# Attention followed by a two-layer product on one core: both transpositions of a unit ahead of both copies, the score stream carried into the next batch, fewer dummy products

## The chip, the cores and the metric

The kernel runs on one core of a Trainium2 chip. Times are device microseconds. A time is the median of several executions. A profile is one further execution, recorded by the hardware profiler; its own time and its span (first to last instruction) are given beside the median. The engines are named PE (TensorE: matrix products), PEld (its weight loads), DVE (VectorE), ACT (ScalarE), POOL (GpSimd) and SP (SyncE); the last two mainly issue transfers here.

## What is computed

Attention with a squared ReLU in place of the softmax, over 8 batches, 12 heads, 448 positions and 64 values a head, and then two matrix products with a squared ReLU between them, on 3,584 rows.

```python
def _attn_ref(q, k, v):                      # (8, 12, 448, 64) each
    S = q.shape[2]
    scale = 1.0 / np.sqrt(q.shape[-1])
    scores = scale * np.matmul(q, k.transpose(0, 1, 3, 2))
    attn = np.maximum(scores, 0.0) ** 2 / S
    return np.matmul(attn, v).astype(np.float32)

def _moe_ref(x, w_in, w_out):                # (3584, 768), (768, 2048), (2048, 768)
    h = x @ w_in
    r = np.maximum(h, 0.0)
    g = r * r
    return (g @ w_out).astype(np.float32)
```

The output of the attention, with heads side by side, is the `x` of the second function.

## The kernel before

**Units and tiles.** A batch is three units of four heads. A unit's keys are cut into seven pieces, so a unit has seven tiles and a batch 21: batch 0 is tiles 0 to 20, batch 1 tiles 21 to 41, and so on. One tile is, for four heads, 64 keys against 448 queries: four score products on PE (line 203, `score`), a ReLU out of PSUM on ACT (line 220 for one tile while the first PSUM layout stands, line 214 for a pair of tiles in the second), a square on DVE (line 230), and four products with v (line 244, `av_round`) which add up over the unit's seven tiles in one PSUM tile `avt`, of which there is a single buffer. At the unit's last tile `avt` is copied to `xt` (line 258 on DVE; for unit 2 line 252 on ACT and line 254 on DVE, a half each). These products with v are called average rounds below.

**Transposing q and k.** Scores need q and k with the head's values on the partitions. For units 0 to 5 PE does it, in `pe_transpose`: 14 transpositions of q into PSUM (line 179), a copy out on DVE (line 186, tile `qT`), then 14 of k and a copy out (tile `kT`). Both halves lie in one PSUM tile, a `slot`. For unit 0 the copy of k is ACT's (line 183). From unit 6 on, q and k are loaded in float32, cast on POOL (line 109) and transposed by a transfer issued from SP (line 121).

**The PSUM layouts.** While batch 0's attention runs, PSUM holds `avt` and three slots of two banks. Then the slots are closed, and two banks `mm` for the products and one score tile `s` of four banks take their place. The later `pe_transpose` calls use that one score tile as their slot.

**Order.** The order is written out by hand. The dummy products (`warm`, line 169: zeros times zeros, 448 columns) come first, with unit 0's transpositions among them. Then batch 0's tiles are run in pairs by `visit`: scores of the pair with their ReLU, then up to three average rounds of earlier tiles, then the squares of the pair. Units 1, 2 and 3 are transposed ahead of pairs 2 and 5 and behind the last. Then come the steps: for each pair of batches, 96 products of the first matrix for either batch (`h_steps`, line 309; ReLU on ACT, line 317, square on DVE, line 320, tile `g`), and 448 products of the second (`o_steps`, line 350). Into this stream of steps `visit` calls and transpositions are set at times of a running clock, as the list `events` says: batch 1's tiles while batch 0's products run, and later batches' likewise. In `h_steps` of batch 0 the first two column groups are sorted so that the parts of `xt` from unit 2 (m of 4 and 5) are used last.

**Loads.** POOL issues the loads that change type on the way (`load16` for q and k, `load_v`, `load_w1`, `load_w2`), in the order of the code. q and k have three buffers each, so unit 3's load waits for unit 0's transpositions, unit 4's for unit 1's.

Of the kernel before, what the change touches and what calls it, by code (L numbers as in the profile page):

```python
# [10 lines left out]
FP16 = mybir.dt.float16  # L11
FP32 = mybir.dt.float32
AF = mybir.ActivationFunctionType
# [4 lines left out]
def kernel(  # L18
# [9 lines left out]
    nc = tc.nc  # L28
# [13 lines left out]
    P = 128  # L42
    J = 7
# [101 lines left out]
    make_identity(nc, ident)  # L145
    zeros = const_p.tile([P, S], FP16, name="zeros", tag="zeros")
    nc.vector.memset(zeros, 0.0)
    load_v(0)
    load16(1)
    load_v(1)  # L150
# [18 lines left out]
            nc.tensor.matmul(ps[:, 0, 0:S], lhsT=zeros[:, 0:P], rhs=zeros,  # L169
                             start=True, stop=True)  # L170

    def pe_transpose(n, fill=0):
        srcs = q16s.pop(n)
        ts = new_qkt()
        ps = slot(FP16)
        for i, (t, src) in enumerate(zip(ts, srcs)):
            for j in range(J):
                for hh in range(2):
                    nc.tensor.transpose(  # L179
                        ps[64 * hh:64 * hh + 64, i, j * P:(j + 1) * P],  # L180
                        src[:, hh, j * D:(j + 1) * D], ident)
            if n == 0 and i == 1:
                nc.scalar.activation(out=t.rearrange("p j c -> p (j c)"),  # L183
                                     in_=ps[:, i, 0:J * P], func=AF.Copy)
            else:
                nc.vector.tensor_copy(  # L186
                    t.rearrange("p j c -> p (j c)"), ps[:, i, 0:J * P])
            if fill:
                warm(fill)
        qkt[n] = ts  # L190


# [88 lines left out]
            load_v(m)  # L281
            dma_transpose(m)

    def visit(tiles, upto, most=3):
        for t in tiles:
            if t % J == 0 and t >= 3 * J:
                enter_unit(t // J)
        at = scores(tiles) if tiles else None
        av_some(upto, most)
        if tiles:  # L290
            square(at, len(tiles))
        av_queue.extend(tiles)
# [4 lines left out]
    def h_steps(b):  # L297
        pr = b // 2
        if b % 2 == 0:
            gts[pr] = []  # L300
        z = (b % 2) * S
        steps = []
        cell: dict = {}

        def step(f, m):
            def run():
                if m == 0:
                    cell[f] = big["mm"].tile([P, 512], FP32, name="hps", tag="mm")
                nc.tensor.matmul(  # L309
                    cell[f][:, 0:S],  # L310
                    lhsT=w1[f // 4][:, m, (f % 4) * P:(f % 4 + 1) * P],
                    rhs=xts[b][:, m, :], start=(m == 0), stop=(m == NM - 1))
                if m == NM - 1:
                    if b % 2 == 0 and f % 2 == 0:
                        gts[pr].append(g_p.tile([P, 2, 2 * S], FP16, name="g", tag="g"))
                    g = gts[pr][f // 2][:, :, z:z + S]
                    nc.scalar.activation(  # L317
                        out=g[:, f % 2], in_=cell[f][:, 0:S], func=AF.Relu)
                    if f % 2 == 1:
                        nc.vector.tensor_mul(g, g, g)  # L320
            return run

        order = [(f, m) for f in range(NF) for m in range(NM)]
        if b == 0:
# [60 lines left out]
        return steps  # L385


    warm(11)
    pe_transpose(0, 3)
    NB0 = NU * J  # L390
    for i in range((NB0 + 1) // 2):
        tiles = [t for t in (2 * i, 2 * i + 1) if t < NB0]
        if i in (2, 5):
            pe_transpose(1 if i == 2 else 2)
        visit(tiles, 2 * (i - 2) + 1)
        if i == 3:
            load16(3)
            load_w1(0)
            load_w1(1)
            load_v(3)  # L400
        if i == 6:
            load16(4)
            load_w1(2)
            load_v(4)
    pe_transpose(3)
    load16(5)
    load_w1(3)
    load_v(5)
    for z in range(4):
        load_w2(z)  # L410
    load_qk(6, nc.gpsimd)
    load_qk(7, nc.gpsimd)
    av_some(NB0, 2)
    first.close()
    for nm, n in (("mm", 2), ("s", 1)):
        big[nm] = ctx.enter_context(tc.tile_pool(name=nm + "ps", bufs=n, space=PSUM))
# [2 lines left out]
    events = []  # L419
# [13 lines left out]
    at0 = T_H + 0.5  # L433
    for pr in range(1, 4):
        t0 = 2 * NB0 * pr
# [14 lines left out]
    for cost, fn in steps:  # L450
        while ev and ev[0][0] <= clock:
            _, tiles, upto = ev.popleft()
            if tiles is None:
                pe_transpose(min(q16s))
            else:
                visit(tiles, upto)
        fn()
        clock += cost
# [30 lines left out]
```

## Time and profile before

| | us |
|---|---|
| median of 3 runs | 422.67 (421.17 to 424.02) |
| the profiled execution, its time | 422.69 |
| its span | 420.9 |
| PE busy | 395.7 (94%) |
| ACT busy | 232.6 (55%) |
| DVE busy | 170.2 (40%) |
| POOL busy | 80.1 (19%) |

PE's busy time counts instructions that are in the array, not how fast they run there: the column for the granted clock says that. An idle time in square brackets at a row's end is the engine's wait ahead of it, with what ended it. Rows of the timeline start with the time from the span's start and the duration; "x14" is a run of fourteen like instructions merged. Matrix products are pipelined, so a run's duration holds the tail of its last one.

### The profile page before, as it was taken

What the parts mean: (1) busy time and instruction counts of PE and PEld (TensorE: products, weight loads), DVE (VectorE), ACT (ScalarE), POOL (GpSimd) and SP (SyncE); (2) the same over time, 40 slices, a digit from 0 to 9 for tenths busy, and PEclk for the clock granted to TensorE, in tenths of its full rate; (3) what the DMA queues carried; (4) which work ended last, traced back from release to release, by engine and by line L of the source; (5) the groups of instructions that cost most, each with busy time, mean ns of one, the idle gap of its engine ahead of it and who ended that gap; (6) DMA issues with size and microseconds to landing.
All of it is one profiled execution on the core that took longest, in us unless ns stands there. A gap on an engine that the chain in (4) does not pass through costs nothing.

```text
span 420.9 us, 7401 instructions
## 1 busy us (share of the span) xinstructions
PE 395.7 (94%) x3193; PEld 199.0 (47%) x3193; DVE 170.2 (40%) x196; ACT 232.6 (55%) x282; POOL 80.1 (19%) x94
## 2 busy tenths in 40 slices
PE   7576769999999999999999999999999999999995
PEld 3332334444555544444555544444555544555663
DVE  0684366554424344556333435655323434320000
ACT  2783657576555566766545567766545566442111
POOL 8545053403030205211011233221000000000000
PEclk9898999999999999999999999999999999999999
DMA  8999989944373988543177886343142210001222
GB/s 128 202 205 206 210 248 240 215 55 121 83 205 62 207 159 182 137 132 66 39 167 168 163 213 153 87 132 65 39 102 56 77 39 0 2 0 38 76 75 76
DMA packets 62496, 50.81 MB, mean 121 GB/s; under 512 B 35712, under 2 KB 58688, under 8 KB 62464
## 3 DMA queue, kind: packets, MB, share of 16 engines
q1 hardware_dynamic: 46752, 33.86, 32.4%
q0 software_dynamic: 15552, 16.39, 24.1%
q8 instruction: 25, 0.41, 0.4%
q10 hardware_dynamic: 160, 0.10, 0.1%
q14 instruction: 7, 0.06, 0.0%
HBM read 45.61 MB, written 11.01 MB: 135 GB/s over the span
## 4 chain that ended last, share of the span: by engine, by line
PE 84%; ACT 12%; DVE 3%; issue 1%; ACTq 0%
PE ops L350 35%; PE hps L309 31%; PE sps L203 9%; PE avt L244 6%; ACT at L214 6%; ACT at L220 4%; ACT g L317 1%; PE slot L169 1%; DVE at L230 1%; DVE qT L186 1%; PE slot L179 1%; PE slot L203 0%; ACT L183 0%; DVE kT L186 0%; DVE g L320 0%
## 5 line engine op out<-in xcount | busy, mean ns | idle before, releaser
L214 ACT ACTIVATE at<-sps 128x1792 f16<-128x1792 f32 (+1 forms) x74 | 122.4, 1654 | 70.1 <-PE sps L203 70.0
L309 PE MATMUL hps<-xt,w 128*128 128x448 f16 x768 | 157.5, 356 | 3.7 <-ACT g L317 2.2
L230 DVE TENSOR_TENSOR at<-at 128x1792 f16<-128x1792 f16 (+1 forms) x95 | 94.7, 1000 | 143.1 <-ACT at L214 136.3
L350 PE MATMUL ops<-w,g 128*128 128x384 f16 x896 | 152.0, 326 | 0.2 <-ACT g L317 0.2
L350 PEld LDWEIGHTS <-g 128*128 128x128 f16 x896 | 85.0, 98 | 66.1 <-issue 12.3
L309 PEld LDWEIGHTS <-w 128*128 128x128 f16 x768 | 71.7, 98 | 85.1 <-issue 25.1
L317 ACT ACTIVATE g<-hps 128x448 f16<-128x448 f32 x128 | 68.4, 543 | 50.2 <-PE hps L309 50.0
L320 DVE TENSOR_TENSOR g<-g 128x896 f16<-128x896 f16 x64 | 46.1, 721 | 34.0 <-ACT g L317 33.4
L109 POOL CAST qs<-qf 128x896 f16<-128x896 f32 x18 | 20.3, 1130 | 184.5 <-DMA qf<-in_q_dram 148.4
L372 ACT ACTIVATE osb<-ops 128x384 f32<-128x384 f32 x55 | 26.9, 490 | 49.5 <-PE ops L350 45.6
L244 PE MATMUL avt<-at,vt 64*64 64x448 f16 x672 | 48.0, 358 | 0.8 <-DVE xt L258 0.6
L203 PE MATMUL sps<-qT,kT 64*64 64x448 f16 x588 | 42.5, 364 | 1.2 <-DVE kT L186 0.7
L258 DVE TENSOR_SCALAR xt<-avt 128x896 f16<-128x896 f32 x23 | 25.0, 1088 | 19.7 <-PE avt L244 19.4
L203 PEld LDWEIGHTS <-kT 64*64 64x64 f16 x672 | 14.2, 106 | 34.0 <-issue 31.3
L244 PEld LDWEIGHTS <-vt 64*64 64x64 f16 x672 | 20.5, 109 | 14.1 <-issue 3.7
L109 POOL CAST ks<-kf 128x896 f16<-128x896 f32 x18 | 23.3, 1296 | 3.7 <-POOL qs L109 2.4
L220 ACT ACTIVATE at<-slot 128x896 f16<-128x896 f32 x21 | 17.3, 946 | 5.5 <-PE slot L203 5.5
L95 POOL DMA_DIRECT2D vt<-in_v_dram x24 | 17.3, 720 | 1.9 <-DMA k<-in_k_dram 1.0
L366 DVE TENSOR_SCALAR osb<-ops 128x192 f32<-128x192 f32 x1 | 0.4, 357 | 35.6 <-ACT osb L363 35.6
L203 PE MATMUL slot<-qT,kT 64*64 64x448 f16 x84 | 7.7, 398 | 3.0 <-ACT at L220 2.0
L179 PEld LDWEIGHTS <-k 128*64 128x64 f16 x84 | 3.4, 118 | 10.8 <-issue 10.8
L179 PE MATMUL slot<-ident,k 128*64 128x128 f16 x56 | 2.7, 243 | 6.1 <-DVE qT L186 6.1
(28 smaller groups left out, 48.0 us busy)
## 6 DMA issues: line engine op xcount, KB each, us to landing
out_dram<-osb SPq DMA_DIRECT2D x54, 192.0 KB, 2.7
qf<-in_q_dram SPq DMA_DIRECT2D x16, 448.0 KB, 4.7
kf<-in_k_dram SPq DMA_DIRECT2D x16, 448.0 KB, 5.4
vt<-in_v_dram POOLq DMA_DIRECT2D x24, 224.0 KB, 4.5
w<-in_moe_w_in_dram POOLq DMA_DIRECT2D x8, 384.0 KB, 11.8
w<-in_moe_w_out_dram POOLq DMA_DIRECT2D x4, 768.0 KB, 17.1
q<-in_q_dram POOLq DMA_DIRECT2D x6, 224.0 KB, 7.1
k<-in_k_dram POOLq DMA_DIRECT2D x6, 224.0 KB, 7.5
```

The source lines that it names most:

```text
L109: nc.gpsimd.tensor_copy(t.rearrange("p j h d -> p h j d"), src.rearrange("p h (j d) -> p h j d", d=D))
L203: nc.tensor.matmul(ps[c, 2 * z + hh, 0:S], lhsT=kT[r, j, c], rhs=qT[r, :, c], start=True, stop=True)
L214: nc.scalar.activation(out=at[:, 0:m], in_=ps[:, 0:m, 0:S], func=AF.Relu, scale=SK)
L220: nc.scalar.activation(out=at[:, 2 * z:2 * z + 2], in_=ps[:, :, 0:S], func=AF.Relu, scale=SK)
L230: nc.vector.tensor_mul(at[:, a:a + step], at[:, a:a + step], at[:, a:a + step])
L244: nc.tensor.matmul(ap[64 * hh:64 * hh + 64, hp, 0:S], lhsT=vt[r, hh, j * D:(j + 1) * D], rhs=at[r, hh, :], start=(j == 0), stop=(j == J - 1))
L258: nc.vector.tensor_scalar(out=xts[b][:, 2 * u:2 * u + 2, :], in0=ap[:, :, 0:S], scalar1=CX, scalar2=None, op0=ALU.mult)
L309: nc.tensor.matmul(cell[f][:, 0:S], lhsT=w1[f // 4][:, m, (f % 4) * P:(f % 4 + 1) * P], rhs=xts[b][:, m, :], start=(m == 0), stop=(m == NM ...
L317: nc.scalar.activation(out=g[:, f % 2], in_=cell[f][:, 0:S], func=AF.Relu)
L320: nc.vector.tensor_mul(g, g, g)
L350: nc.tensor.matmul(cell[0][:, 0:HALF], lhsT=gts[pr][f // 2][:, f % 2, tb * P:(tb + 1) * P], rhs=w2[f // 4][:, f % 4, hf * HALF:(hf + 1) * ...
L372: nc.scalar.activation(out=cell[1][:, z:z + HALF], in_=cell[0][:, 0:HALF], func=AF.Copy, scale=CO)
```

## The change

- `pe_transpose` transposes q and k both, and then copies both. For unit 0 alone each copy still follows its own transpositions, and k gets a slot of its own; the dummies around unit 0 are 10, 1 and 1, and were 11, 3 and 3.
- ACT gets a one-column activation of `zeros` at the program's start.
- `visit` can call `pe_transpose` itself, between a pair's scores and its average rounds (`turn`). Units 1, 2 and 3 are transposed at pairs 1, 4 and 7.
- The first loop runs over 11 full pairs, so tile 21, the first of batch 1, goes through with tile 20. The loads that stood at pairs 3 and 6 and behind the loop stand at pairs 0, 2 and 5.
- The events of batch 0's products are laid out anew: the rest of batch 0's average rounds, then pairs 11 to 20 with units 4 and 5 transposed ahead of pairs 13 and 16, then two lots of average rounds.
- The sorted order of the first column groups holds for batch 1 as well.

```diff
+    junk = const_p.tile([P, 1], FP16, name="junk", tag="junk")
+    nc.scalar.activation(out=junk, in_=zeros[:, 0:1], func=AF.Relu)
...
-    def pe_transpose(n, fill=0):
+    def pe_transpose(n):
...
+        def copy(i):
+            dst = ts[i].rearrange("p j c -> p (j c)")
+            if n == 0 and i == 1:
+                nc.scalar.activation(out=dst, in_=ps[:, i, 0:J * P], func=AF.Copy)
+            else:
+                nc.vector.tensor_copy(dst, ps[:, i, 0:J * P])
+
+        for i, src in enumerate(srcs):
+            if n == 0 and i == 1:
+                ps = slot(FP16)
             for j in range(J):
...
-            if fill:
-                warm(fill)
+            if n == 0:
+                copy(i)
+                warm(1)
+        if n > 0:
+            copy(0)
+            copy(1)
...
-    def visit(tiles, upto, most=3):
+    def visit(tiles, upto, most=3, turn=None):
...
         at = scores(tiles) if tiles else None
+        if turn is not None:
+            pe_transpose(turn)
         av_some(upto, most)
...
-        if b == 0:
+        if b < 2:
             order.sort(key=lambda fm: (fm[0] // 2, fm[1] >= 4, fm)
...
-    warm(11)
-    pe_transpose(0, 3)
+    warm(10)
+    pe_transpose(0)
     NB0 = NU * J
-    for i in range((NB0 + 1) // 2):
-        tiles = [t for t in (2 * i, 2 * i + 1) if t < NB0]
-        if i in (2, 5):
-            pe_transpose(1 if i == 2 else 2)
-        visit(tiles, 2 * (i - 2) + 1)
-        if i == 3:
+    for i in range(11):
+        visit([2 * i, 2 * i + 1], 2 * (i - 2) + 1, turn={1: 1, 4: 2, 7: 3}.get(i))
+        if i == 0:
             load16(3)
...
-        if i == 6:
+        if i == 2:
             load16(4)
...
-    pe_transpose(3)
-    load16(5)
...
-    av_some(NB0, 2)
+        if i == 5:
+            load16(5)
...
-    events.append((0.7, [NB0, NB0 + 1], NB0))
-    for i in range(1, 11):
-        tiles = [NB0 + t for t in (2 * i, 2 * i + 1) if t < NB0]
-        events.append((2.0 + i * (T_H - 4.5) / 10.5, tiles, NB0 + 2 * (i - 2) + 1))
-    for i in range(3):
-        events.append((T_H - 2.2 + 0.7 * i, [], 2 * NB0))
-    for t in (1.9 + 2.5 * (T_H - 4.5) / 10.5, 1.9 + 6 * (T_H - 4.5) / 10.5):
-        events.append((t, None, 0))
-    events.sort(key=lambda e: e[0])
+    seq = [11, 12, -4, 13, 14, 15, -5, 16, 17, 18, 19, 20]
+    events.append((1.5, [], NB0 - 1))
+    for z, i in enumerate(seq):
+        at = 2.0 + z * (T_H - 5.0) / 11
+        if i < 0:
+            events.append((at, None, -i))
+        else:
+            events.append((at, [2 * i, 2 * i + 1], 2 * (i - 2) + 1))
+    events.append((T_H - 1.6, [], 39))
+    events.append((T_H - 0.3, [], 41))
```

What this does to the order, engine by engine. A row is one instruction, with its line, its output and input tiles and the output's size, or several like ones in a row ("x4"). DVE from the program's start to unit 2's transpositions, before (`at` are scores, `qT` and `kT` the transposed q and k):

```order
L186 COPY qT<-slot 128x896
L230 TENSOR_TENSOR at<-at 128x896 x4
L186 COPY qT<-slot 128x896
L186 COPY kT<-slot 128x896
L230 TENSOR_TENSOR at<-at 128x896 x6
```

The same place after:

```order
L184 COPY qT<-slot 128x896
L240 TENSOR_TENSOR at<-at 128x896 x2
L184 COPY qT<-slot 128x896
L184 COPY kT<-slot 128x896
L240 TENSOR_TENSOR at<-at 128x896 x6
```

Unit 1's two copies moved ahead of the squares of tiles 2 and 3.

DVE over the end of batch 0's stream, before (`xt` is the copied average, the last of these rows the square of a pair in the second PSUM layout):

```order
L258 TENSOR_SCALAR xt<-avt 128x896
L230 TENSOR_TENSOR at<-at 128x896 x5
L186 COPY qT<-slot 128x896
L186 COPY kT<-slot 128x896
L254 TENSOR_SCALAR xt<-avt 128x448
L230 TENSOR_TENSOR at<-at 128x1792
```

And after, from unit 3's copies on:

```order
L184 COPY qT<-slot 128x896
L184 COPY kT<-slot 128x896
L240 TENSOR_TENSOR at<-at 128x896 x2
L268 TENSOR_SCALAR xt<-avt 128x896
L240 TENSOR_TENSOR at<-at 128x896 x6
L264 TENSOR_SCALAR xt<-avt 128x448
L240 TENSOR_TENSOR at<-at 128x1792
```

Unit 3's copies moved from behind the last square of batch 0 to eight squares ahead of the stream's end, which now has one square more.

ACT from the program's start into batch 0's product, before:

```order
L183 ACT_TABLE_LOAD
L183 ACTIVATE kT<-slot 128x896
L220 ACTIVATE at<-slot 128x896 x21
L214 ACTIVATE at<-sps 128x1792
L252 ACTIVATE xt<-avt 128x448
```

And after:

```order
L149 ACT_TABLE_LOAD
L149 ACTIVATE junk<-zeros 128x1
L182 ACTIVATE kT<-slot 128x896
L230 ACTIVATE at<-slot 128x896 x22
L262 ACTIVATE xt<-avt 128x448
```

The table load moved to the one-column activation, the stream has 22 single tiles, and the copy to `xt` no longer stands behind a pair's ReLU.

More of the change, by code (lines that the diff above doesn't have):

```diff
@@ L175, in pe_transpose @@
         ps = slot(FP16)
-        for i, (t, src) in enumerate(zip(ts, srcs)):
+        def copy(i):
[7 more added lines that the diff above has]
+                ps = slot(FP16)
             for j in range(J):
@@ L181, in pe_transpose @@
                         src[:, hh, j * D:(j + 1) * D], ident)
[L182 to L187, printed above, removed]
-            if fill:
-                warm(fill)
+            if n == 0:
[4 more added lines that the diff above has]
+            copy(1)
         qkt[n] = ts
@@ L404 @@
             load_v(4)
-    pe_transpose(3)
-    load16(5)
[L407 to L412, printed above, removed]
-    av_some(NB0, 2)
+        if i == 5:
+            load16(5)
+            load_w1(3)
+            load_v(5)
+            for z in range(4):
+                load_w2(z)
+            load_qk(6, nc.gpsimd)
+            load_qk(7, nc.gpsimd)
     first.close()
@@ L453 @@
             if tiles is None:
-                pe_transpose(min(q16s))
+                pe_transpose(upto)
             else:
```

## The prediction

> **What bounds the kernel now.** I read the chain that ended last first, then the busy time by stretch, then the timeline of the first 78 us. The page's chain has two engines in it:
>
> ```profile
> PE 84%; ACT 12%; DVE 3%; issue 1%; ACTq 0%
> ```
>
> Cutting the span where the program changes stage (batch 0's attention; its first product; batch 1's first product; the rest) shows where PE is not full. Columns are the stretch, its length, then busy us and instruction counts by engine, the granted TensorE clock, the DMA share and GB/s:
>
> ```profile
> 0.00:34.60 34.60, 22.96 (x293) 11.51 (x293) 19.12 (x31) 19.53 (x23) 21.03 (x35) 0.95 1.14 180
> 34.60:77.40 42.80, 35.75 (x325) 15.91 (x326) 23.85 (x26) 25.04 (x27) 15.28 (x18) 0.92 1.09 226
> 77.40:102.00 24.60, 23.64 (x173) 10.46 (x171) 11.61 (x15) 17.74 (x23) 5.97 (x7) 1.00 0.62 126
> 102.00:420.90 318.90, 313.36 (x2404) 161.11 (x2403) 115.64 (x125) 170.34 (x210) 37.82 (x36) 1.00 0.44 100
> ```
>
> PE is idle for 11.6 us of the first stretch and 7.1 us of the second, and part of both runs at half clock (0.95 and 0.92). From 77.4 us PE is 96 to 98% busy at full clock. The edits end there, and the order on every engine behind that point is what it was, but for six products in batch 1's first group. So the sum is how much earlier batch 1's product, or the first score pair behind it (77.92 us before), can start.
>
> **Part 1, the start (fewer dummy products, early table load).** Rows of PE and ACT, then the issue of k and its time to landing:
>
> ```profile
> 6.26 1.18 PE L169 MATMUL slot<-zeros 128*128 128x448 f16 x3
> 7.08 1.28 ACT L183 ACT_TABLE_LOAD   x1 [7.08 <-DVE qT L186]
> 7.37 0.58 PE L179 MATMUL slot<-ident,k 128*64 128x128 f16 x14
> 8.38 0.92 ACT L183 ACTIVATE kT<-slot 128x896 f16<-128x896 f16 x1
> 9.35 0.76 PE L203 MATMUL slot<-qT,kT 64*64 64x448 f16 x12 [0.72 <-ACT kT L183]
> 9.78 3.35 ACT L220 ACTIVATE at<-slot 128x896 f16<-128x896 f32 x4 [0.49 <-PE slot L203]
> 2.07 0.72 POOL L90 DMA_DIRECT2D k<-in_k_dram  x1
> k<-in_k_dram POOLq DMA_DIRECT2D x1, 224.0 KB, 4.1
> ```
>
> k is there at 2.07 + 4.1 = 6.17 us; PE comes to it at 7.37, behind three dummies of 0.39 each; ACT's copy then waits for the table load until 8.36. After: the load stands first on ACT and is over before 6 us. One dummy ends at 6.26 + 0.39 = 6.65. The 14 k transpositions then take 0.58 (this row) or, still at half clock, 0.96 (a row below); I take 0.96, as the dummies just ahead run at half clock. So 7.6, copy 0.92, first scores at 8.6 and not 9.35: 0.7 gained. Bounds: 1.1 with the 0.58, and 0 if the clock comes so late that scores crawl too.
>
> **Part 2, batch 0's scores.** DVE's and ACT's groups between 9.7 and 32.1 us, and PE's transpositions of unit 1:
>
> ```profile
> L230 DVE TENSOR_TENSOR at<-at 128x896 f16<-128x896 f16 x20 | 12.2, 624 | 6.7 <-ACT at L220 6.6
> L258 DVE TENSOR_SCALAR xt<-avt 128x896 f16<-128x896 f32 x2 | 2.2, 1088 | 0.1
> L186 DVE COPY kT<-slot 128x896 f16<-128x896 f16 x2 | 1.2, 624 | 1.7 <-PE slot L179 1.7
> L220 ACT ACTIVATE at<-slot 128x896 f16<-128x896 f32 x21 | 17.3, 946 | 5.5 <-PE slot L203 5.5
> 11.56 0.58 PE L179 MATMUL slot<-ident,q 128*64 128x128 f16 x14 [0.42 <-ACT at L220]
> 14.37 0.96 PE L179 MATMUL slot<-ident,k 128*64 128x128 f16 x14 [2.23 <-DVE qT L186]
> ```
>
> Before, k's transpositions wait 2.23 us for the copy of q, which itself stands behind four squares on DVE; ACT runs dry (5.5 us in all) and PE falls to half clock (0.96 for 0.58). After, 28 transpositions run together, one tile pair ahead of use, and behind two squares, so ACT keeps its cadence (3.35/4 = 0.84 a tile). What is late next is DVE: it was idle 6.7 us waiting for ACT, and now has no pause. ACT starts tile 0 at 8.6 + 0.43 (9.78 − 9.35) = 9.05 and tile 1 ends at 10.75, which frees the slot for the transpositions; they end 2 × 0.58 later, at 11.9. From there DVE has, in its order, six copies of 0.62 (3.7), twenty squares of 0.624 (12.5) and two x copies of 1.09 (2.2): 18.4, plus some 0.4 before unit 3's copies, so its last square of the stream (tile 21) ends at 30.7. At half clock the 28 take 1.92, and all is 0.8 later. ACT needs 22 × 0.82 = 18 us from 9.05, 27 us, so it is no longer the bound. The copies wait on DVE ahead of the squares of the pair they were issued with; queued behind them are those squares, and PE's average rounds wait for these a visit later.
>
> **Part 3, into the first product.** The rows from the end of batch 0's attention:
>
> ```profile
> 24.58 0.76 PE L244 MATMUL avt<-at,vt 64*64 64x448 f16 x12 [0.17 <-DVE xt L258]
> 38.91 0.54 ACT L252 ACTIVATE xt<-avt 128x448 f16<-128x448 f32 x1
> 39.48 0.62 DVE L254 TENSOR_SCALAR xt<-avt 128x448 f16<-128x448 f32 x1 [4.92 <-ACT xt L252]
> 40.16 0.73 PE L309 MATMUL hps<-xt,w 128*128 128x448 f16 x3 [0.31 <-DVE xt L254]
> 42.37 0.57 PE L203 MATMUL sps<-qT,kT 64*64 64x448 f16 x8
> ```
>
> The new PSUM pools are free when ACT is through with tile 21, at about 29.9 (its scores stand behind average rounds that wait for the second x copy, 27.2, and go through ACT as the last two of 0.82). Eight products (seven take 1.50, a row below) then reach 31.5, twelve average products of 0.76 reach 32.2 (tile 20's square is done at 30.1), ACT's x copy 32.8, DVE's 33.4: the place of 40.16 before. Two products on, the next score pair starts at 33.9, against 42.37: 8.5 gained so far, of which 0.7 is part 1. Seven of its nine products in that place now stand behind the pair; the loop of part 4 has to hold them.
>
> **Part 4, the pairs of batch 1.** One 4-bank score buffer makes a loop: PE scores, ACT's 1.66, and so on.
>
> ```profile
> 44.71 0.57 PE L203 MATMUL sps<-qT,kT 64*64 64x448 f16 x8 [0.34 <-ACT at L214]
> 50.08 0.57 PE L203 MATMUL sps<-qT,kT 64*64 64x448 f16 x8
> 50.70 1.66 ACT L214 ACTIVATE at<-sps 128x1792 f16<-128x1792 f32 x1 [0.35 <-PE sps L203]
> 50.96 1.50 PE L309 MATMUL hps<-xt,w 128*128 128x448 f16 x7
> 52.42 0.57 PE L203 MATMUL sps<-qT,kT 64*64 64x448 f16 x8
> 54.75 0.57 PE L203 MATMUL sps<-qT,kT 64*64 64x448 f16 x8
> 60.01 0.58 PE L179 MATMUL sps<-ident,k 128*64 128x128 f16 x14 [2.35 <-DVE qT L186]
> ```
>
> (The loop is 52.42 − 50.08 = 2.34.) The next rows are those of the same loop at its end:
>
> ```profile
> 61.31 0.57 PE L203 MATMUL sps<-qT,kT 64*64 64x448 f16 x8 [0.71 <-DVE kT L186]
> 62.90 2.62 PE L309 MATMUL hps<-xt,w 128*128 128x448 f16 x7
> 65.45 0.57 PE L203 MATMUL sps<-qT,kT 64*64 64x448 f16 x8
> 72.55 0.38 PE L203 MATMUL sps<-qT,kT 64*64 64x448 f16 x4
> 77.92 0.57 PE L203 MATMUL sps<-qT,kT 64*64 64x448 f16 x8
> ```
>
> Before, nine intervals take 72.55 − 42.37 = 30.2: two hold transpositions (5.37 from 44.71, 6.56 from 54.75), and one after the 2.35 wait runs at half clock (61.31 to 65.45, 4.14; seven products 2.62 and not 1.50). After, there are nine intervals too: seven of 2.34, and two with both transpositions. Such a one is the score pair 0.62, ACT 1.66, 28 transpositions 1.16, a square of the product (line 320, 0.6) on DVE ahead of the copies, two copies 1.25: 5.3 to 5.4, so 27.1 in all. The gain there is 3.1. PE's work in an interval (0.4 scores, 0.5 averages, six or seven products, 2.3) is just covered. The last pair starts at 33.9 + 27.1 = 61.0. Behind it stand 28 average products (1.75) and 18 products (3.4) beside 0.4 of scores, 5.55 us, where there were 5.37. The first pair of batch 2 starts at 66.55: 77.92 − 66.55 = 11.4 gained. Reordering batch 1's first two groups moves unit 5's x copy (1.09) behind eight products: nothing lost.
>
> **Part 5, the loads.** POOL's order is unchanged row for row; only where the code stands moved, so the queue fills and drains as before. Unit 5's k, issued at 25.93, lands 10.1 later, at 36.0; its transpositions come at about 48.8. The price is 0. What is near is unit 6, whose transposed k batch 2's first pair needs:
>
> ```profile
> 60.42 2.43 SPq L121 DMA_TRANSPOSE kT<-ks  x1
> kT<-ks SPq DMA_TRANSPOSE x18, 4.2
> ```
>
> Its loads are set by the queue, not by PE: 60.42 + 4.2 = 64.6, two us ahead of my 66.55. So no gain beyond 13.2 can show.
>
> **The sum.** The profiled execution took 422.69 us, span 420.9, the same as the median of the runs, 422.67. 422.7 − 11.4 = 411.3. I add 0.9: half of the 1.8 (4.14 − 2.34) that one 3.4 us stretch at half clock costs on the loop, for I can't say where such a stretch falls. Forecast 412.2.
>
> **The clock, weighed.** The trace: dummies 0.39 each up to 7.4, then 0.58 for 14 transpositions. The Trainium skill (TensorE: Matmul & The Clock Gate, Part 1) has the clock doubled after one busy window of about 3.4 us, free-running, and its Part 4 says that transpose-mode work doesn't count as busy. By that rule this change is at risk, since it takes five dummies from the window that ended near 7.2. By the rule the sum would be the 414 of rival (a), by the row, with transpositions at full clock right behind dummies, 411.3; no run here yet shows how transpositions count.
>
> **Rivals.** (a) Clock late: dummies fewer, so half clock until about 14 us. Price: 0.7 of part 1 halves, 28 transpositions 1.92 for 1.16, scores and averages of some four tiles doubled: 1.5 to 2, so 414. For it: the dummies removed were the last ones; against it: eleven earlier ones remain but for one. Chance 0.12. (b) Batch 0 doesn't tighten: PE stops at the single average buffer, ACT and DVE take turns, and the stream lasts as long as before (32.1). Price 3 us of part 2 and 3: 415.3. For it: DVE is now full, and each x copy blocks PE; chance 0.15. (c) Further gain up to unit 6's transposed k: 409.5; chance 0.08. (d) Slower: with DVE and ACT pacing PE in batch 0, its activity stays under what raises the clock, and half clock lasts into the first product. A product then costs 2.62/7 and not 1.50/7, 0.16 more; 71 of batch 0's 96 would have to run so to eat 11.4, and all 96 give 411.3 + 15.4 = 426.7. Against it: PE was busier than in the stretch before, where the clock returned after one window each time. Chance 0.03. (e) It doesn't do what it says: the copies of q and k still serialise with PE, since tiles are tracked whole; then parts 2 and 4 gain half: 417; chance 0.05.
>
> **How the numbers follow.** The forecast, 410.5 to 413.8 (no stretch, or one and a little), has 0.57. Range 409 to 416.5 takes in (a), (b) and (c), 0.92 with the forecast, of which I take off 0.1 for a term that is sized wrongly. A difference of 1%, 4.2 us, is what a measurement can tell here. Faster by over 1% (below 418.4): 0.94; within: 0.03; slower: 0.03.
>
> **What would show it.** First scores near 8.6; no wait of PE for a q copy; ACT's 22 activations without 2 us pauses; DVE without pause from 12 to 31; score pairs 2.34 apart; first pair of batch 2 at 66.5; everything behind shifted alike. Wrong would be: half clock beyond 10 us, a pair interval over 5.5 with transpositions, or batch 2's first pair waiting for a load.

## The result and the profile after

| | us |
|---|---|
| before, median of 4 runs | 423.35 (421.17 to 425.57) |
| after, median of 4 runs | 411.98 (411.19 to 413.03) |
| ratio, with its 95% interval | 0.9733 [0.9674, 0.9791] |
| the profiled execution of after, its time | 413.03 |
| its span | 411.3 |

The change makes the kernel 2.7% faster, and the median lies 0.2 us below the forecast of 412.2. The profiled execution is the slowest of the four. In it the chain that ended last has a second large part, transfers, where before it had ACT:

```profile
PE 79%; DMA 14%; ACT 4%; POOL 2%; issue 1%; DVE 0%; POOLq 0%
```

The busy time of after, cut at its first product, at batch 2's first score pair, at the place where its order has settled, and at the end (columns as in the prediction):

```profile
0.00:27.51 27.51, 19.24 (x284) 9.91 (x285) 17.71 (x32) 20.86 (x25) 16.18 (x28) 1.00 1.10 173
27.51:66.85 39.34, 33.12 (x331) 15.12 (x330) 22.70 (x28) 24.80 (x27) 14.71 (x18) 1.00 1.11 216
66.85:92.36 25.51, 24.64 (x170) 10.76 (x170) 12.68 (x14) 17.35 (x22) 11.40 (x12) 0.94 1.06 227
92.36:411.30 318.94, 313.36 (x2404) 161.11 (x2403) 118.48 (x125) 170.30 (x210) 37.10 (x37) 1.00 0.45 100
```

By the clock column, which reads 1.00 ahead of its first change whatever the clock is there, the first two stretches run at 1.00, where before had 0.95 and 0.92. PE is still idle for 27.51 − 19.24 = 8.3 us and 39.34 − 33.12 = 6.2 us of them. The last stretch, 318.94 us, is as long as before's last one (318.90) and has the same 2404 products: all that was gained was gained ahead of it. There is one stretch at half clock, in the third row (0.94).

The timeline of after, PE and ACT, from the first scores into the loop of batch 1:

```profile
0.73 1.28 ACT L149 ACT_TABLE_LOAD   x1 [0.73 <-PEq L482]
7.76 0.76 PE L213 MATMUL slot<-qT,kT 64*64 64x448 f16 x12 [0.72 <-ACT kT L182]
8.20 3.35 ACT L230 ACTIVATE at<-slot 128x896 f16<-128x896 f32 x4 [0.49 <-PE slot L213]
11.88 8.46 ACT L230 ACTIVATE at<-slot 128x896 f16<-128x896 f32 x10 [0.34 <-PE slot L213]
20.57 6.90 ACT L230 ACTIVATE at<-slot 128x896 f16<-128x896 f32 x8 [0.22 <-PE slot L213]
27.51 1.67 PE L321 MATMUL hps<-xt,w 128*128 128x448 f16 x8 [1.13 <-ACT at L230]
31.65 0.57 PE L213 MATMUL sps<-qT,kT 64*64 64x448 f16 x8
33.99 0.57 PE L213 MATMUL sps<-qT,kT 64*64 64x448 f16 x8 [0.53 <-ACT at L224]
39.06 0.57 PE L213 MATMUL sps<-qT,kT 64*64 64x448 f16 x8 [0.52 <-DVE kT L184]
```

ACT's 22 activations of the stream stand in three runs with gaps of 0.33 and 0.23 us between them; the pauses of 2 us are gone. DVE in the same place, two copies and a run of squares of the timeline:

```profile
11.56 0.62 DVE L184 COPY qT<-slot 128x896 f16<-128x896 f16 x1 [0.98 <-PE slot L191]
12.10 0.61 DVE L184 COPY kT<-slot 128x896 f16<-128x896 f16 x1
24.79 3.33 DVE L240 TENSOR_TENSOR at<-at 128x896 f16<-128x896 f16 x6
```

And the groups of after in the window from 7.7 to 28.2 us (busy us, mean ns, then idle time and what ended most of it):

```profile
L240 DVE TENSOR_TENSOR at<-at 128x896 f16<-128x896 f16 x22 | 12.4, 619 | 3.0 <-ACT at L230 3.0
L230 ACT ACTIVATE at<-slot 128x896 f16<-128x896 f32 x22 | 18.5, 924 | 1.3 <-PE slot L213 1.1
```

DVE still waits 3.0 us for ACT here, and ACT only 1.3 us for anything. A single square lasts 0.62, but a run of six takes 3.33, so 0.55 each: neighbours overlap. The timeline of after at the end of batch 1's loop:

```profile
58.14 0.57 PE L213 MATMUL sps<-qT,kT 64*64 64x448 f16 x8
58.69 1.51 POOL L109 CAST qs<-qf 128x896 f16<-128x896 f32 x1 [15.26 <-DMA qf<-in_q_dram]
61.99 1.23 SPq L121 DMA_TRANSPOSE kT<-ks  x1
63.08 0.93 PE L321 MATMUL hps<-xt,w 128*128 128x448 f16 x4
66.85 0.96 PE L213 MATMUL sps<-qT,kT 64*64 64x448 f16 x8 [2.85 <-DMA kT<-ks]
67.75 3.01 PE L321 MATMUL hps<-xt,w 128*128 128x448 f16 x9
72.61 0.57 PE L213 MATMUL sps<-qT,kT 64*64 64x448 f16 x8
```

PE is through at 63.08 + 0.93 = 64.01 and then stands for 2.85 us until unit 6's transposed k is there. Behind the wait the clock is halved: eight scores take 0.96 and not 0.57, and the interval to the next pair is 72.61 − 66.85 = 5.76, where before's was 4.38 (77.92 to 82.30 in its timeline). So the account of the profiled execution is 77.92 − 66.85 = 11.07 gained up to the pair, 1.38 given back behind it: 422.69 − 9.69 = 413.0, and it took 413.03.

### The profile page after: what moved, and what is told of

Its sections match the earlier page's. It is cut to its first block, busy times and chain, and to the rows that moved or that the text cites. A ratio compares the mean times of both kernels' runs of the same rounds, so it can differ in the third digit from the quotient of the medians.

```text
span 411.3 us, 7394 instructions
## 1 busy us (share of the span) xinstructions
PE 390.4 (95%) x3188; PEld 196.9 (48%) x3188; DVE 171.6 (42%) x196; ACT 233.3 (57%) x283; POOL 79.4 (19%) x94
## 4 chain that ended last, share of the span: by engine, by line
PE 79%; DMA 14%; ACT 4%; POOL 2%; issue 1%; DVE 0%; POOLq 0%
PE ops L362 36%; PE hps L321 29%; PE sps L213 8%; PE avt L254 5%; DMA qf<-in_q_dram 5%; DMA w<-in_moe_w_in_dram 3%; ACT at L224 3%; DMA k<-in_k_dram 2%; DMA q<-in_q_dram 2%; DMA kT<-ks 1%; ACT g L329 1%; POOL vt L95 0%; POOL k L90 0%; POOL qs L109 0%; POOL q L89 0%
## 5 line engine op out<-in xcount | busy, mean ns | idle before, releaser
L224 ACT ACTIVATE at<-sps 128x1792 f16<-128x1792 f32 x73 | 121.5, 1664 | 63.6 <-PE sps L213 63.4
L362 PEld LDWEIGHTS <-g 128*128 128x128 f16 x896 | 85.0, 98 | 66.1 <-issue 12.3
L332 DVE TENSOR_TENSOR g<-g 128x896 f16<-128x896 f16 x64 | 47.7, 746 | 32.0 <-ACT g L329 31.4
L254 PE MATMUL avt<-at,vt 64*64 64x448 f16 x672 | 46.9, 350 | 2.6 <-DVE xt L268 2.4
L109 POOL CAST ks<-kf 128x896 f16<-128x896 f32 x18 | 22.1, 1229 | 3.9 <-POOL qs L109 2.0
L230 ACT ACTIVATE at<-slot 128x896 f16<-128x896 f32 x22 | 18.5, 924 | 1.3 <-PE slot L213 1.1
L132 POOL DMA_DIRECT2D w<-in_moe_w_in_dram x8 | 5.3, 666 | 3.4 <-DMA w<-in_moe_w_in_dram 1.2
L171 PE MATMUL slot<-zeros 128*128 128x448 f16 x12 | 4.6, 542 | 1.2 <-DVE zeros L147 1.2
```

The source lines that it names most:

```text
L109: nc.gpsimd.tensor_copy(t.rearrange("p j h d -> p h j d"), src.rearrange("p h (j d) -> p h j d", d=D))
L224: nc.scalar.activation(out=at[:, 0:m], in_=ps[:, 0:m, 0:S], func=AF.Relu, scale=SK)
L230: nc.scalar.activation(out=at[:, 2 * z:2 * z + 2], in_=ps[:, :, 0:S], func=AF.Relu, scale=SK)
L254: nc.tensor.matmul(ap[64 * hh:64 * hh + 64, hp, 0:S], lhsT=vt[r, hh, j * D:(j + 1) * D], rhs=at[r, hh, :], start=(j == 0), stop=(j == J - 1))
L362: nc.tensor.matmul(cell[0][:, 0:HALF], lhsT=gts[pr][f // 2][:, f % 2, tb * P:(tb + 1) * P], rhs=w2[f // 4][:, f % 4, hf * HALF:(hf + 1) * ...
```

## The experiments

All kernels compute the whole reference; none leaves work out. The runs fall into groups, and each group has its own runs of the kernel before beside it, so between groups it is the ratio or the difference to these that is compared. A is the reading that unit 6's transposed k is the cap behind which gains vanish, where not said otherwise.

**The start.** The old dummies back and no early activation:

```diff
-    junk = const_p.tile([P, 1], FP16, name="junk", tag="junk")
-    nc.scalar.activation(out=junk, in_=zeros[:, 0:1], func=AF.Relu)
...
-                warm(1)
+                warm(3)
...
-    warm(10)
+    warm(11)
```

> The changed kernel with the start of the kernel before: 11, 3 and 3 dummies, no one-column activation, so that the table load waits again. In the changed kernel's trace PE waits 2.85 us at batch 2's first score pair (66.85 us) for unit 6's transposed k, a transfer. Theory A (that wait sets the end of the stage): the start is 1.3 to 1.6 us later (first scores at 9.1 to 9.35, not 7.76) and the wait shrinks by as much; the time stays within 0.5 us of the changed kernel. Theory B (the terms add up): the time is 1.3 to 1.6 us longer.

412.76 (410.08 to 413.30), ratio 0.9777 [0.9745, 0.9808]: no difference from the change itself that these runs can tell. First scores came at 8.03. The table load did not go back: it stood at 0.73 us as in after, because k's own slot takes away the wait that had held ACT's first instruction. So the edit undid less than meant, and what it did undo was 8.03 − 7.76 = 0.27 us at the first scores. That is no more than one and the same start varies by: the second profile of the changed kernel, below, has its first scores at 7.99. Batch 2's first pair again came right upon the transposed k (wait 0.36).

**The copies.** The copy of q goes back between the two transpositions, in the changed kernel:

```diff
         for i, src in enumerate(srcs):
+            if n > 0 and i == 1:
+                copy(0)
...
         if n > 0:
-            copy(0)
             copy(1)
```

> The changed kernel, but with q's copy again between q's and k's transpositions of units 1 to 5; places and stream stay. Theory A: each of the five costs one q copy with its handoffs on PE (0.7 us), 3.5 us in all, of which the 2.85 us wait for unit 6 takes up most: 0.3 to 1 us more than the changed kernel. Theory B (the waits of the kernel before come back whole, 2.23, 2.23, 1.62, 1.08 and 2.35 us, 9.5 in all, less 2.85): 6 to 7 us more.

415.07 (413.96 to 417.24), ratio 0.9853 [0.982, 0.9887]: 5.8 us below before, where the changed kernel was 11.4 and 9.3 below it in its two groups, so a third to a half of the gain is lost, between the two expectations. In its timeline PE waits for the copy of q again, 1.4 us in batch 0 and twice some 1.6 in batch 1, and at batch 2's first pair no longer for a load:

```profile
41.99 0.58 PE L193 MATMUL sps<-ident,k 128*64 128x128 f16 x14 [1.62 <-DVE qT L184]
...
71.97 0.57 PE L214 MATMUL sps<-qT,kT 64*64 64x448 f16 x8
```

The copy's waits sum to 4.7, of which after's 2.85 for the load are to be taken off: 1.8. Three of its runs at a granted clock of 1.00 took 413.96 to 414.35; runs of the changed kernel at that clock took 411.44 and 411.96: 2.0 to 2.9, across groups. The other three runs have lower clocks; the profiled one of them holds three stretches at half clock (0.988).

**The copies alone**, in the kernel before, all else as it was:

```diff
+            if n > 0:
+                continue
...
+        for i in range(2 if n > 0 else 0):
+            nc.vector.tensor_copy(
+                ts[i].rearrange("p j c -> p (j c)"), ps[:, i, 0:J * P])
```

> The kernel before with one part of the change alone: for units 1 to 5 q and k both transposed, then both copied, at the old places. Theory A (the wait of PE for q's copy is most of the gain): the waits of 2.23, 2.23, 1.62, 1.08 and 2.35 us go, the next wait takes up a third: 4 to 6 us less than the kernel before. Theory B (place and stream matter, since PE then waits for both copies at once where they stand right ahead of use): 1 to 2.5 us less.

413.94 (413.73 to 414.05), ratio 0.9806 [0.9781, 0.9832], 8.2 us below before and more than either theory expected. Its busy time, in two stretches:

```profile
0.00:34.00 34.00, 23.68 (x316) 11.97 (x317) 19.04 (x33) 21.52 (x25) 20.46 (x34) 1.00 1.13 179
34.00:78.00 44.00, 38.32 (x360) 17.35 (x362) 27.29 (x30) 29.38 (x34) 15.71 (x17) 1.00 1.14 225
```

And those of before, cut at the same times:

```profile
0.00:34.00 34.00, 22.56 (x289) 11.51 (x293) 18.56 (x31) 19.53 (x23) 20.45 (x34) 0.95 1.14 180
34.00:78.00 44.00, 36.75 (x339) 16.09 (x335) 24.41 (x27) 25.58 (x28) 16.08 (x18) 0.92 1.09 227
```

27 and 21 instructions more on PE in the same time, at a clock of 1.00 for 0.95 and 0.92. Before had three stretches of 3.4 us at half clock in there, this kernel's profiled run has none. At 1.8 us each (the prediction's 4.14 − 2.34) an estimated 5.4 of the 8.2 at most is the clock's and 2.8 at least the waits'. The share isn't settled closer: that the waits that went are the reason for the clock too is likely, not shown. Nor does a lower mean clock always cost time, for two of this kernel's four runs had 0.990 and took 413.86 and 413.73, no longer than the two at 1.000 (414.05 and 414.02). Here PE waits for no load: batch 2's first pair stands at 69.23, beyond the landing of the transposed k.

**The stream.** The changed kernel with the old end of batch 0's stream and the old events; and beside it the changed kernel once more.

```diff
-        visit([2 * i, 2 * i + 1], 2 * (i - 2) + 1, turn={1: 1, 4: 2, 7: 3}.get(i))
+        visit([t for t in (2 * i, 2 * i + 1) if t < NB0], 2 * (i - 2) + 1, turn={1: 1, 4: 2, 7: 3}.get(i))
...
+    av_some(NB0, 2)
...
+    events.append((0.7, [NB0, NB0 + 1], NB0))
+    for i in range(1, 11):
...
-                pe_transpose(upto)
+                pe_transpose(min(q16s))
```

> The changed kernel with batch 0's stream ending at tile 20 again, and the old layout of batch 1's pairs and of units 4 and 5; start, order of copies and the places of units 1 to 3 stay. Theory A (the stream across the batches is worth one interval of 2.34 us, less what of it lay under the wait for unit 3's copy): 1.5 to 3 us more than the changed kernel, or, where the wait for unit 6 takes it up, 0 to 1.5. Theory B (the stream's layout is most of the gain of the stretch behind 34 us): 4 us more or over.

> The changed kernel as it is, beside the other runs of this call. Both theories: 410.5 to 412.5 us. Its trace shows how far the wait for unit 6's transposed k (2.85 us in the first trace, 0.36 with the start undone) swings between executions.

Stream undone: 412.91 (411.88 to 413.06), ratio 0.9777 [0.975, 0.9804]. The changed kernel: 412.87 (411.40 to 415.72), ratio 0.9776 [0.9747, 0.9805]. The same time. The first pair of batch 2 came at 68.11 without a wait in the one and at 68.55 behind a wait of 3.27 for the transposed k in the other: the cap swallows most of what the stream brings. (In the first, part of the 68.11 is a half-clock stretch at 27.1 to 30.5.) What the stream is worth is seen better when the cap is gone, below: the pair then stands at 64.55, 3.6 earlier, of which that stretch can explain 1.8.

**The cap: unit 6 loaded ahead of the weights.** POOL issues the loads of units 6 and 7 behind four loads of the second matrix. Here they go first:

```diff
         if i == 5:
...
-            for z in range(4):
-                load_w2(z)
             load_qk(6, nc.gpsimd)
             load_qk(7, nc.gpsimd)
+            for z in range(4):
+                load_w2(z)
```

> The changed kernel with the four loads of the second matrix issued behind those of q and k of units 6 and 7, not ahead of them. Theory A: the wait of 2.85 us goes, and the half-clock stretch that follows it in that trace with it (another 1.3 us): 2.9 to 4.2 us less than the changed kernel, first pair of batch 2 at 64.0. Theory B (later waits take up what is won here, for example for the second matrix, now last in the queue): within 0.5 us of the changed kernel, with PE waiting on a transfer behind 64 us.

411.09 (410.52 to 413.35), ratio 0.9763 [0.9733, 0.9792]; the 3 to 4 us of theory A did not come. Batch 2's first pair no longer waits, but it stands at 67.31. The timeline of this kernel says why:

```profile
45.56 6.79 SPq L121 DMA_TRANSPOSE kT<-ks  x1
45.82 3.12 DVE L240 TENSOR_TENSOR at<-at 128x1792 f16<-128x1792 f16 x1
46.18 0.94 POOL L109 CAST qs<-qf 128x896 f16<-128x896 f32 x1
47.06 0.94 POOL L109 CAST ks<-kf 128x896 f16<-128x896 f32 x1
50.60 0.96 PE L213 MATMUL sps<-qT,kT 64*64 64x448 f16 x8 [2.54 <-DVE kT L184]
```

POOL's casts of unit 7 now fall into the interval in which unit 5 is transposed. The square ahead of the two copies on DVE takes 3.12 us, where a pair's square takes 1.09, and PE waits 2.54 for the copy of k. The wait for a load was exchanged for a wait behind a cast. With the old dummies beside the same edit (the start's edit and this one together):

> Both edits together: the transfers out of the way, and the start of the kernel before. Theory A: the start now shows its worth, 1.3 to 1.6 us more than the kernel with the transfers out of the way alone. Theory B (the start is worth nothing anywhere): the same as that kernel within 0.4 us.

410.52 (409.63 to 410.82), ratio 0.9733 [0.9706, 0.976]: the same wait (2.40), but no half-clock stretch behind it in the profiled run. The old start cost nothing here (theory B). The two loads of units 6 and 7 parted, so that the casts stand elsewhere:

```diff
-            for z in range(4):
-                load_w2(z)
+            load_w2(0)
+            load_w2(1)
             load_qk(6, nc.gpsimd)
+            load_w2(2)
+            load_w2(3)
             load_qk(7, nc.gpsimd)
```

> The changed kernel with q and k of unit 6 loaded behind two of the four loads of the second matrix, unit 7 behind all four. When both were ahead, unit 6's and 7's casts on POOL fell on the transpositions of unit 5, where a square on DVE then took 3.12 us and not 1.09. Theory A (the wait for unit 6 and that collision are what is left to win): no wait at batch 2's first pair, which starts at 63.5 to 64.5 us, no square over 2 us in an interval with transpositions, and 1 to 3 us less than the changed kernel. Theory B (the casts slow DVE wherever they fall, and PE with it): the wait is gone but the first pair is no earlier than 66, and the time is the same within 0.5 us.

410.22 (409.77 to 414.34), ratio 0.9745 [0.9706, 0.9784]; two of the six runs took over 413. No collision, but still a wait of 1.74 for the transposed k, though its cast was eight us earlier than in after. The view of transfers has the time from issue to landing of that one transposition. In after:

```profile
kT<-ks SPq DMA_TRANSPOSE x1, 4.8
```

With unit 6 first:

```profile
kT<-ks SPq DMA_TRANSPOSE x1, 19.4
```

With the loads parted:

```profile
kT<-ks SPq DMA_TRANSPOSE x1, 12.3
```

With unit 6 first and the old start it is 19.2. Issued at 61.99, 45.56, 53.26 and, in the last, 45.84, they land at 66.8, 65.0, 65.6 and 65.0. However early the transposition is issued, it comes at about 65, when most of what POOL had queued is through (the last weights landed at 64.7 and 64.9 with unit 6 first, the last of unit 7's k at 63.2 with the loads parted).

It does not stand idle until then. The view of transfers of unit 6 first, from 54.97 to 60.00, has for each queue its packets, their MB and their time as a share of 16 engines; q0 holds POOL's loads, q1 SP's transfers, here mainly the transpositions of unit 6:

```profile
q0 software_dynamic: 588, 0.88, 95.3%
q1 hardware_dynamic: 581, 0.14, 21.7%
```

The two queues move as many packets as each other, but a packet of POOL's loads holds 1.5 KB here and one of SP's 0.24 KB. So a transposition, which is all small packets, gets through slowly as long as large ones are queued beside it. To go first in POOL's order isn't enough; fewer loads must be in the queue, which the next kernel tests.

**The cap removed.** Two of the four weight loads are issued behind unit 7's casts instead:

```diff
+        if n == 5:
+            load_w2(2)
+            load_w2(3)
...
-            for z in range(4):
-                load_w2(z)
+            load_w2(0)
+            load_w2(1)
```

> The changed kernel with the last two of the four loads of the second matrix issued behind unit 7's casts, not ahead of unit 6's loads. With unit 6 merely in the middle of the queue its k was cast at 53.2 us, but the transposition issued at 53.26 landed 12.3 us later, at 65.6, when the loads queued ahead of it were through. Theory A (the transposition waits behind whatever load was issued ahead of it, so that the bytes in the queue and not unit 6's place set its end): 1.5 MB fewer lie ahead, unit 6's transposed k lands by 60, PE has no wait for it, batch 2's first pair starts at 63.5 to 64.5 us, and the time is 408 to 409.5. Theory B (a transposition of this kind takes some 10 us beside any traffic): it still lands behind 64 and the time is that of the changed kernel.

410.01 (409.39 to 410.15), ratio 0.973 [0.971, 0.9751], 11.0 us below before. Its timeline:

```profile
53.13 1.25 SPq L121 DMA_TRANSPOSE kT<-ks  x1
64.55 0.57 PE L213 MATMUL sps<-qT,kT 64*64 64x448 f16 x8
```

And its view of transfers:

```profile
kT<-ks SPq DMA_TRANSPOSE x1, 5.5
```

The transposed k, issued at nearly the same time as with the loads parted, lands at 58.6 and not 65.6, and PE comes to the pair at 64.55 without waiting: 4.0 us ahead of the second profile of the changed kernel and 2.3 ahead of the first. From 53.13 to 58.60 the queues moved:

```profile
q1 hardware_dynamic: 1707, 0.65, 57.7%
q0 software_dynamic: 278, 0.23, 39.8%
```

So theory A's landing, pair and missing wait came true, and in the profiles 2.3 to 4.0 us are what the cap took. In the time it shows less: the ratio is 0.973, where the changed kernel had 0.9733 and 0.9776 with wider intervals, and the 408 to 409.5 that theory A named was missed by half a microsecond.

**ACT or DVE?** To the same kernel, unit 2's copy of k given to ACT: `if n in (0, 2) and i == 1:`.

> The kernel of the two later loads, and unit 2's k copied by ACT (0.92 us) and not by DVE (0.62). Theory A (DVE is the bound of batch 0's stream, as the prediction had it): the first product starts 0.5 us earlier, time 0 to 0.5 less than with the later loads alone. Theory B (ACT, with 22 tiles of 0.82, is as near): the first product starts up to 0.9 us later, time 0 to 0.9 more.

409.92 (408.77 to 412.77), ratio 0.9739 [0.9709, 0.977]: no difference in time. The first product came at 28.89 and not 27.62, but this profiled run had a half-clock stretch at 10.3 to 13.7 and first scores 0.3 later. The interval that holds the moved copy lies behind that stretch, from unit 2's transpositions of q to unit 3's. Without the edit:

```profile
15.39 0.58 PE L191 MATMUL slot<-ident,q 128*64 128x128 f16 x14 [0.43 <-ACT at L230]
20.75 0.58 PE L191 MATMUL slot<-ident,q 128*64 128x128 f16 x14
```

With it:

```profile
16.14 0.58 PE L191 MATMUL slot<-ident,q 128*64 128x128 f16 x14 [0.43 <-ACT at L230]
22.02 0.58 PE L191 MATMUL slot<-ident,q 128*64 128x128 f16 x14 [0.43 <-ACT at L230]
```

That is 5.88 for 5.36, at a granted clock of 1.00 in both, and the interval is 5.35 or 5.36 in every other kernel that has this order. So 0.92 more on ACT cost 0.52, and 0.62 less on DVE gained nothing: ACT sets the pace there, as theory B has it, though the half microsecond doesn't show in the median.

**The dummies.** The kernel without the cap, with the old number of dummies (11, 3 and 3) and the early table load kept:

```diff
-                warm(1)
+                warm(3)
...
-    warm(10)
+    warm(11)
```

> The kernel of the two later loads, with 11, 3 and 3 dummies again; the one-column activation stays. Theory A (the dummies behind unit 0's transpositions only stand in the way): first scores 0.3 to 0.7 us later, and as much more in the time. Theory B (they keep the clock up): the same time or less, with fewer executions that hold a half-clock stretch; the mean granted clock of the runs is then nearer to 1 than without them.

409.21 (408.99 to 409.23), ratio 0.9712 [0.9689, 0.9734], 11.8 us below before. All five runs lie below all five of the kernel without the cap, by 0.8 at the median, though the intervals of the two ratios overlap. Their granted clocks were 0.998 to 1.000, those of the other 0.996 in four runs of five, which fits one stretch of 3.4 us in 408. The first scores came 0.2 later (8.19 and not 7.96), the first product 0.1 earlier (27.49 and not 27.62). Unit 1's k says why an earlier start is worth so little. PE comes to its transpositions ahead of the load, in after and in its second profile:

```profile
10.94 0.58 PE L191 MATMUL slot<-ident,k 128*64 128x128 f16 x14 [0.38 <-DMA k<-in_k_dram]
12.22 0.58 PE L191 MATMUL slot<-ident,k 128*64 128x128 f16 x14 [1.44 <-DMA k<-in_k_dram]
```

With the old dummies, here and with the start undone, there is no such wait, and the first product came at 27.49 and 27.33, where after's came at 27.51. So fewer dummies gained nothing that shows; with the one-column activation, without which the table load stood at 0.73 too, they are the part of the change that can be undone. This version has the lowest median and the lowest ratio of all that ran.

## Why the prediction was right, and where it was not

The time was right within a us, and the largest mechanism with it: PE's waits for the copies of q went, and with them most of the gain. Two of its terms were wrong and offset each other, so that the time came out this close is in part luck.

| step | forecast, us | after |
|---|---|---|
| first scores | 8.6 | 7.76 |
| first product | 29.9 | 27.51 |
| first pair of the loop | 33.9 | 31.65 |
| nine intervals of batch 1 | 27.1 | 58.14 − 31.65 = 26.5 |
| last pair to PE free for batch 2 | 5.55 | 64.01 − 58.14 = 5.87 |
| wait for unit 6's transposed k | 0 | 2.85 |
| batch 2's first pair | 66.55 | 66.85 |
| half clock behind it | 0.9 | 1.38 |

**Part 1** was right in kind and 0.8 us short, outside its own bound of 1.1 (9.35 − 7.76 = 1.59). The clock rose earlier than allowed for: the 14 k transpositions took 0.58 and not the 0.96 that I chose. Their start was 6.17, not 6.65, for the sum left out that one dummy fewer stands ahead of q's transpositions as well (5.04 and not 5.37), and these took 0.65 and not 0.96. With the old dummies the first scores came at 8.03, 8.19 and 8.42, with few at 7.76 to 8.26; the bulk is the early table load, which came with k's own slot even where the one-column activation was left out. And what is won ahead of 8.2 ends at unit 1's k, a load that the prediction gave no price.

**Part 2** named the wrong engine, and DVE's pauses, 3.0 us of waiting for ACT, did not go as it said. "What is late next is DVE" rested on 18.4 us summed from single durations, and in a run a square or a copy takes 0.55 (24.79 and 11.56 above), not 0.62. DVE had 3.0 us to spare and ACT 1.3, so ACT, at 0.84 a tile, set the end: 8.20 + 22 × 0.84 = 26.7 and its gaps. The copy that was moved from DVE to ACT says the same. The forecast of 27 for ACT was nearer to the first product, 27.51, than the 29.9 that I took. Against the forecast, 1.55 of these 2.4 us are the DVE term and 0.85 the start.

**Part 3 and part 4** held. The loop is 2.34; a transposing interval is 39.06 − 33.99 = 5.07, where 5.3 to 5.4 was said; neighbours on DVE overlap there too, which explains most of it.

**Part 5** was wrong in both its numbers. "60.42 + 4.2 = 64.6" took the issue time from before and the median of all 18 transpositions. In after the loads started 1.5 us later and the transposition was issued at 61.99; it took 4.8 and landed at 66.8. The page's median was a bad price, since unit 6's own transposition had taken 5.3 in before. So the claim that the landing is two us ahead of PE failed by 2.2 on its own side and by 2.5 on PE's: PE was free at 64.0, and batch 2's first pair waited for a load, which the prediction had named as a sign of being wrong. Rival (c), "further gain up to unit 6's transposed k", had the right mechanism, and its cap came into play, only later than it said: at 66.85, which by chance is the time I had forecast for PE without it. Removing the cap moved that pair to 64.55, so both halves of the coincidence are shown.

**The half-clock allowance** was 0.9 for one stretch at an unknown place; there was one, right behind the wait, and it cost 1.38.

**The rivals.** (a) fell for the first rise of the clock: in the eight profiles with fewer dummies it came between 5.1 and 6.9 us, in the five with the old number between 5.1 and 7.2. (Of the five dummies that the prediction took from the window near 7.2, two stood behind it, at 7.88.) But half clock beyond 10 us, another of its signs of being wrong, came in three of those eight, the second profile of the changed kernel among them (13.1 to 16.5), and in none of the four that have the old dummies with both transpositions ahead of the copies; what fewer dummies risk is open. (b) and (d) fell: batch 0 tightened, and its first product ran at full clock in both profiles of the changed kernel. (The price of (b) should have been 412.2 + 3 = 415.2.) (e) fell: no PE row of after waits for a copy of q; and the copies' order turned out to be the strongest part, 8.2 us alone, 5.8 left without it. These two together are 14.0, more than the 9.3 and 11.4 that the changed kernel gained in its two groups. Part of the difference is the cap, for the kernel without it gained 11.0, with the dummies back 11.8; what else the parts share isn't accounted for.

**Open** stay the clock's share in the 8.2 us, what the removed cap is worth in time beyond the noise, why the cap's landing differs by 1.7 us between two profiles of the same kernel, and whether DVE would have set batch 0's pace had ACT been faster.

## What to carry to other kernels

A copy that PE waits for in the middle of its own work can cost twice: the wait, and then a clock that is halved behind it; let PE do all it can before the first copy, one step ahead of use. When a gain of this size moves work towards a transfer, price that transfer by its own issue and its own landing, not by a median over all of its kind, and look at what else is in the queue at that moment, and in packets of what size. Sum a busy engine's work by runs of neighbouring instructions, not by single durations.

## What the runs showed of the hardware

- **A transposition by transfer shares the transfer engines with the loads queued beside it, packet by packet.** 128x896 elements took 4.8 to 6.3 us from issue to landing with little queued, 12.3 and 19.4 with more of POOL's loads (768 KB of weights each among them) still under way, and landed at 65.0 to 65.6 in each of those cases. The Trainium skill (DMA: Bandwidth & Descriptors, "Queues, rings and completion order") says that each transfer engine takes turns between the queues that have work, a packet at a time. The trace of unit 6 first agrees: 588 packets of one queue and 581 of the other in the same 5.03 us, of 1.5 and 0.24 KB. The counts aren't equal everywhere (739 and 424 with the loads parted, from 53.26 to 59.50), and what held SP's queue back there is open. By the size of its packets the 224 KB of one transposition are an estimated 930 packets, so equal turns leave it far behind loads of larger packets.
- **Casts on POOL hold up DVE's square.** 3.12 us with two casts of 0.94 beside it, 1.09 without: the difference, 2.03, is near the sum of the two casts, 1.88. The Trainium skill (SBUF — State Buffer, "SBUF: two separate sides") says that a DVE operation with two SBUF inputs and a POOL operation that reads SBUF exclude one another for the whole instruction. The lengths agree with it; by the recorded starts, though, the square began 0.36 before the first cast, so which of them held the port isn't shown. In after both orders are seen: a cast that began 0.36 behind a square took 1.51 and not 0.93 (58.69), and a square that began 0.30 behind a cast took 1.57 and not 1.09.
- **Transpositions count for the clock.** The Trainium skill (TensorE: Matmul & The Clock Gate, Part 4) says that they don't count as busy the same way, and the prediction weighed that. In the kernel with unit 2's copy on ACT (first window below) PE had dummies until 5.07, one more at 6.03 of 0.56, and transpositions:

```profile
3.46:6.87 3.41, 3.34 (x28) 1.55 (x28) 0.62 (x1) 0.00 (x0) 3.41 (x6) 1.00 1.22 186
```

  In before (second window) it had 2.61 us of dummies and nothing else:

```profile
0.36:3.77 3.41, 2.61 (x8) 1.06 (x9) 0.24 (x1) 0.00 (x0) 2.53 (x8) 1.00 0.27 22
```

  The clock column reads 1.00 in both, so it says nothing before the first change; durations do. Fourteen transpositions across the end of the first window take 0.73, and the twelve scores behind them 0.76, as at full clock; behind the second window fourteen took 0.96. The first window had 1.61 + 0.56 = 2.2 us of dummies, less than the second, and raised the clock. So here transpositions counted. The edges of these windows are inferred from later changes of the clock, 3.41 us apart.
- **A stretch at half clock often follows a wait, and lasts 3.4 us.** In after it came behind the wait of 2.85, in its second profile behind 3.27 and 6.9 long, in the kernel with unit 6 first behind 2.54. It did not behind 2.40 with the old start, and in the kernel with unit 2's copy on ACT it came (10.3 to 13.7) behind 3.42 us in which PE was busy for 1.82 and no single wait was over 0.72. So a wait of this size is a risk, not a rule.
